# Keys and queries in pieces of two tiles, with scores from the first piece on

## The chip, the cores and the metric

The kernel runs on one core of a Trainium2 chip. The metric is the device time of one execution in microseconds; the time of a kernel is the median of its runs. The profile is one execution recorded by the hardware profiler.

## The reference

Three stages follow one another. The first is attention in blocks: 2 batches, 8 heads, 768 rows, head size 64. Each block of 32 query rows sees 8 memory rows of its own head and the keys from 16 before the block to 8 behind it.

```python
for c in range(nc):
    q_c = q[:, :, c_start:c_end]
    k_full = np.concatenate([mem_k, k[:, :, l_start:r_end]], axis=2)
    v_full = np.concatenate([mem_v, v[:, :, l_start:r_end]], axis=2)
    scores = scale * np.matmul(q_c, k_full.transpose(0, 1, 3, 2))
    a = np.exp(scores - np.max(scores, axis=-1, keepdims=True))
    a = a / (np.sum(a, axis=-1, keepdims=True) + 1e-09)
    out[:, :, c_start:c_end] = np.matmul(a, v_full)
```

Its output, as 1536 rows of 512, goes through a mixture of eight experts with two experts a row (512 to 1024 to 512, with noise on the logits), and that through a second one with one expert a row and a capacity of 384 rows. All arithmetic is in float32.

## The kernel before, in words

The order of the work is written out by hand; the engines run their instructions in the order of the program, and waits stand where data demands it. The attention treats twelve tiles of 128 rows, six a batch. The loop at L1486 calls `step(t, units)` for t from -2 to 11. Step t computes the scores of tile t+2 and subtracts their maxima (`scores`, `submax`), turns the differences of tile t+1 and takes their exponentials (`prob`), multiplies tile t with V (`attend`, `normalise`), transposes the rows of tile t-1 (`x_tr`) and makes the gate logits of tile t-2 (`logits`). Ahead of each step the loop stores the rows of the tile before (`put_x`) and issues what the table `ahead` holds for that step.

Queries and keys are needed with the head dimension on the partitions. A piece (`load_qk`, L121) is loaded by the SyncE queue, 512 KB in one transfer. Two "units" (`t_unit`, L218) turn a piece: four 128x128 transposes on TensorE into a PSUM bank, and then the copies of `t_put` (L233) into `qz` or `kt`, where the rows are put in the order in which the score matmuls read them. Q is copied by ScalarE, K by VectorE. In the kernel before, a piece is 1024 consecutive rows of four heads laid end to end (8 rows, 2 KB, a partition); four heads of 768 rows are three pieces, and a tile of all heads needs all three. So all six loads of batch 0 and their twelve units stand ahead of the first score (L1429 to L1436), and the twelve units of batch 1 are taken off a list within steps 0 to 3, as many as the table `UP` says (half of them ahead of the probabilities, half behind `normalise`). The raw pieces have six buffers.

V is loaded in groups of 128 rows with 256 B runs (`load_v`). GpSimd copies a second arrangement of it, shifted by 32 rows (`v_odd`), and the memory rows are put beside it by copies (`v_mem`) or by small transfers (`v_odd` with a queue). `v_blank` and `blank` clear what is never written. The memory keys are multiplied into place by `mem_keys`. The value matmuls of tile t (L309) read all of this for their group.

`fill` and `half_step` let the routing of the first expert stage go forward a step at a time on VectorE; it begins after step 5. At step 6 the buffers of batch 0 are given up and the first weights are loaded there (`whole0`, `PIECES`). `ZEROS` and `ZT` say ahead of which step rows of the buffers in memory are set to zero. After the attention come the expert jobs, a list of units with background work between them, up to the end of the kernel.

## Time and profile before

| What | Value |
|---|---|
| Runs (us) | 604.55, 601.17, 604.13 |
| Median (us) | 604.13 |
| The profiled execution's own time (us) | 603.3 |
| Its span (us) | 601.5 |
| TensorE busy | 581.5 us (97%) |
| VectorE busy | 370.2 us (62%) |
| ScalarE busy | 304.2 us (51%) |
| GpSimd busy | 169.8 us (28%) |
| Moved | 110.39 MB, mean 184 GB/s |

The span goes from the first to the last instruction that the profiler recorded; what of the execution lies around it is the difference to its own time. Engines are named PE (TensorE matmul), PEld (TensorE weight load, beside PE), DVE (VectorE), ACT (ScalarE), POOL (GpSimd) and SP (SyncE). A q behind the name is the engine's queue of instructions. In a row such as `psB<-ident,raw` the written tile stands first, and L223 is line 223 of the kernel. A bracket at the end of a row of the timeline gives the idle time of the engine just before it and what ended it.

### The profile page before, as it was taken

How to read it: one execution, taken by the hardware profiler on the slowest of the kernel's cores; microseconds unless marked ns; L12 is line 12 of the kernel's file. 1: busy time of each engine (PE TensorE's matmuls, PEld its weight loads, DVE VectorE, ACT ScalarE, POOL GpSimd, SP SyncE). 2: the span in 40 equal slices, each digit the busy share in tenths (PEclk: the TensorE clock that was granted, in tenths of full speed). 3: DMA queues.
4: the chain of work that ended last, by engine and by line, in shares of the span. 5: the costliest groups of instructions: out<-in, count | busy, mean ns of one | idle time of the engine just before them, and what ended most of it. 6: DMA issues, size and time to landing. Idle time of an engine off the chain costs nothing. (4 is left out here: it accounts for less than half of the span.)

```text
span 601.5 us, 12261 instructions
## 1 busy us (share of the span) xinstructions
PE 581.5 (97%) x4528; PEld 518.4 (86%) x4540; DVE 370.2 (62%) x986; ACT 304.2 (51%) x641; POOL 169.8 (28%) x244
## 2 busy tenths in 40 slices
PE   7899999999999999999999999999999999999995
PEld 4788756889999999999998898988979979878974
DVE  7788766877555555555556256373758648357571
ACT  5764633355445445445355345344327657367562
POOL 8896104135113114213040311212351111220102
PEclk9999999999999999999999999999999999999998
DMA  9996747475856758546465664554377576975741
GB/s 247 289 197 160 249 138 236 118 239 148 273 158 137 223 158 200 175 135 167 141 121 166 138 162 147 103 148 103 40 246 237 171 262 225 390 274 170 250 158 42
DMA packets 75373, 110.39 MB, mean 184 GB/s; under 512 B 28099, under 2 KB 28099, under 8 KB 75306
## 3 DMA queue, kind: packets, MB, share of 16 engines
q1 hardware_dynamic: 65866, 84.72, 45.4%
q0 software_dynamic: 9440, 24.81, 17.7%
q8 instruction: 38, 0.62, 0.4%
q14 instruction: 29, 0.24, 0.1%
HBM read 88.90 MB, written 20.48 MB: 182 GB/s over the span
## 5 line engine op out<-in xcount | busy, mean ns | idle before, releaser
L784 DVE TENSOR_TENSOR wlo<-raww,whi 128x512 fp32r<-128x512 f32 x226 | 150.2, 688 | 39.1 <-ACT whi L783 37.6
L783 ACT ACTIVATE whi<-raww 128x512 fp32r<-128x512 f32 x228 | 135.5, 623 | 5.6 <-SPq L1354 2.7
L861 DVE SCALAR_TENSOR_TENSOR hl<-psA,hh 128x256 fp32r<-128x256 f32 (+7 forms) x104 | 53.3, 513 | 75.1 <-ACT hh L860 68.9
L860 ACT ACTIVATE hh<-psA 128x256 fp32r<-128x256 f32 (+7 forms) x104 | 47.2, 454 | 99.0 <-PE psA L849 91.5
L849 PE MATMUL psA<-xh,wlo 128*128 128x256 f32 (+7 forms) x416 | 84.8, 325 | 1.5 <-issue 0.7
L849 PE MATMUL psA<-xl,whi 128*128 128x256 f32 (+7 forms) x416 | 82.2, 319 | 0.0
L849 PE MATMUL psA<-xh,whi 128*128 128x256 f32 (+7 forms) x416 | 82.2, 319 | 0.0
L1026 POOL DMA_INDIRECT x_rows<-yr,ids x25 | 39.2, 1567 | 125.5 <-ACT whi L783 82.1
L849 PEld LDWEIGHTS psA<-xh,wlo 128*128 128x128 f32 x416 | 66.4, 188 | 3.8 <-issue 1.2
L849 PEld LDWEIGHTS psA<-xl,whi 128*128 128x128 f32 x416 | 68.1, 188 | 0.5 <-DVEq L1262 0.2
L849 PEld LDWEIGHTS psA<-xh,whi 128*128 128x128 f32 x416 | 68.1, 188 | 0.3
L789 POOL DMA_INDIRECT xg<-x_rows,ids x37 | 37.4, 1010 | 109.3 <-DVE gs L1066 44.6
L849 PE MATMUL psC<-wlo,hh 128*128 128x512 f32 (+1 forms) x184 | 52.6, 406 | 0.0
L849 PE MATMUL psC<-whi,hh 128*128 128x512 f32 (+1 forms) x184 | 50.8, 395 | 0.0
L849 PE MATMUL psC<-whi,hl 128*128 128x512 f32 (+1 forms) x184 | 50.5, 394 | 0.0
L801 DVE TENSOR_TENSOR xl<-psB,xh 128x512 fp32r<-128x512 f32 (+4 forms) x33 | 21.1, 640 | 39.1 <-ACT xh L800 39.0
L849 PEld LDWEIGHTS psC<-whi,hh 128*128 128x128 f32 (+1 forms) x184 | 34.0, 186 | 8.4
L849 PEld LDWEIGHTS psC<-whi,hl 128*128 128x128 f32 (+1 forms) x184 | 34.1, 186 | 8.0
L800 ACT ACTIVATE xh<-psB 128x512 fp32r<-128x512 f32 (+4 forms) x33 | 18.3, 556 | 40.2 <-PE psB L797 37.7
L849 PE MATMUL psA<-hh,wlo 128*128 128x312 f32 (+4 forms) x160 | 36.9, 351 | 0.8 <-DVE hl L861 0.5
L1033 POOL DMA_INDIRECT out_dram<-yr,oids x12 | 12.0, 1000 | 87.5 <-ACT yr L1004 47.7
L849 PEld LDWEIGHTS psC<-wlo,hh 128*128 128x128 f32 (+1 forms) x184 | 31.9, 186 | 5.5
(366 smaller groups left out, 927.1 us busy)
## 6 DMA issues: line engine op xcount, KB each, us to landing
raww<-in_moe_w_dram SPq DMA_DIRECT2D x114, 512.0 KB
raw<-in_k_dram SPq DMA_DIRECT2D x6, 512.0 KB
raw<-in_q_dram SPq DMA_DIRECT2D x6, 512.0 KB
x_rows<-xs SPq DMA_DIRECT2D x12, 256.0 KB
out_dram<-zero SPq DMA_DIRECT2D x3, 1024.0 KB
x_rows<-zero POOLq DMA_DIRECT2D x5, 520.0 KB
v<-in_v_dram SPq DMA_DIRECT2D x10, 256.0 KB
whi<-in_moe_w_dram SPq DMA_DIRECT2D x4, 512.0 KB
```

Source lines behind the costliest of these rows:

```text
L783: nc.scalar.activation(hi[:, c], raw, AF.Copy)
L784: (eng or nc.vector).tensor_tensor(lo[:, c], raw, hi[:, c], op=OP.subtract)
L789: return nc.gpsimd.indirect_dma_start(out=xg, out_offset=None, in_=src, in_offset=bass.IndirectOffsetOnAxis(ap=ids_ap, axis=0))
L800: nc.scalar.activation(xh[:, :, o], pv[:, :, 0:n], AF.Copy)
L801: low = lambda: nc.vector.tensor_tensor(xl[:, :, o], pv[:, :, 0:n], xh[:, :, o], op=OP.subtract)
L849: nc.tensor.matmul(ps, w[a], x[b], start=first and i == 0, stop=last and i == n - 1)
L860: nc.scalar.activation(hh[:, f, 0:C], ps[:, 0:C], AF.Relu)
L861: nc.vector.scalar_tensor_tensor(hl[:, f, 0:C], ps[:, 0:C], 0.0, hh[:, f, 0:C], op0=OP.max, op1=OP.subtract)
L1026: wr = nc.gpsimd.indirect_dma_start(out=x2_d, out_offset=off, in_=yr[:n], in_offset=None, compute_op=OP.add)
L1033: wr = nc.gpsimd.indirect_dma_start(out=out, out_offset=off, in_=yr[:n, 0:DM], in_offset=None, bounds_check=N - 1, oob_is_err=False)
```

## The change

A piece is now 256 rows of all eight heads, which is two tiles, with two rows (512 B) of each head on a partition. Three pieces make a batch as before, at 512 KB each, but the scores of tile 0 and 1 need the first Q piece and the first and second K pieces alone. A unit turns four heads. Its copies are shared: half x = 0 goes to ScalarE, x = 1 to VectorE, and a K unit has four copies of 64x256 in place of two of 64x512.

Ahead of the first score stand the units of K0, Q0 and K1, and the memory keys. All other units are in the list and are taken within steps -1 to 7, two a step (three in step 3, with the memory keys of batch 1). The loads come in the order K0, memory keys, Q0, K1, memory values, V groups 0 and 1, Q1, V 2, K2, Q2, V 3, and then batch 1; the V groups of batch 1 are issued in steps 1 to 4 instead of ahead of the loop, and their second arrangement is made in steps 4 to 9 instead of 2 to 6. Raw pieces have four buffers, and two more for the last pieces of batch 1 in the other pool. The memory values of group 1 go from ScalarE to GpSimd, and one clearing of `qz` of batch 1 from GpSimd to ScalarE. The zero rows move to steps 5, 6 and 7.

```diff
-UP = (0, 0, 4, 4, 4, 1)
+UP = ((0, 0), (0, 2), (2, 0), (2, 0), (2, 0), (3, 0), (2, 0), (2, 0), (2, 0), (2, 0))
...
-RB = 6
+RB = 4
...
-ZEROS = {0: 1, 1: 1}
+ZEROS = {6: 1, 7: 1}
...
-ZT = 2
+ZT = 5
...
-        t = a0p.tile([128, 2, 8 * D], F32, name="raw", bufs=RB)
-        nc.sync.dma_start(t, bass.AP(tensor=src.tensor, offset=src.offset + (b * H * S + 1024 * i) * D,
-                                     ap=[[8 * D, 128], [HP * S * D, 2], [1, 8 * D]]))
+        last = (b, i) == (1, 2)
+        t = (asp if last else a0p).tile([128, H, 2 * D], F32, name="raw_" if last else "raw", bufs=2 if last else RB)
+        nc.sync.dma_start(t, bass.AP(tensor=src.tensor, offset=src.offset + (b * H * S + 256 * i) * D,
+                                     ap=[[2 * D, 128], [S * D, H], [1, 2 * D]]))
...
-    for w in (1, 0):
-        load_qk(0, 0, w)
+    load_qk(0, 0, 1)
     nc.sync.dma_start(memk, mem_k.rearrange("b h m d -> (b h m) d"))
-    for i in (1, 2):
-        for w in (1, 0):
-            load_qk(0, i, w)
+    load_qk(0, 0, 0)
+    load_qk(0, 1, 1)
...
+    nc.scalar.activation(qz[1][64:128, :, 0, :], warmer[64:128, None, 0:32].to_broadcast([64, HP * NC, 32]), AF.Copy)
...
-        nc.gpsimd.memset(qz[b][64:128, :, 0, :], 0.0)
+        if b == 0:
+            nc.gpsimd.memset(qz[b][64:128, :, 0, :], 0.0)
...
+        for h in range(HP):
+            nc.tensor.transpose(p[:, 128 * h:128 * h + 128], src[:, HP * a + h], ident)
...
+            act = x == 0 or (b, i, which, a) == (0, 0, 0, 1)
+            put = act_copy if act else nc.vector.tensor_copy
             if which == 0:
+                to = qz[b].rearrange("p (h c) a n -> p h c a n", h=HP)[o, :, 8 * i:8 * i + 8, a]
+                put(to.rearrange("p h c (n x) -> p x h c n", x=2)[:, x], pr)
             else:
+                for u in range(2):
+                    j = 320 * i + 16 + 24 * u + x
+                    to = kt[b][o, j:j + 1]
+                    put(bass.AP(tensor=to.tensor, offset=to.offset, ap=[list(to.ap[0]), [KW, HP], [40, 8], [2, 8]]),
+                        pr[:, :, :, 8 * u:8 * u + 8])
+            if not act:
                 fill()
...
-        some((n + 1) // 2)
+        some(n[0])
         pe_part()
-        if 0 <= t + 1 < NT:
+        if 0 <= t + 1 < NT and t:
             prob(t + 1)
         if on:
             attend(t)
             normalise(t, end)
-        some(n // 2)
+        some(n[1])
+        if t == -1:
+            prob(1)
...
+    for u in range(2):
+        t_unit(0, 0, 1, u, "BC"[u])
+    mem_keys(0)
+    for u in range(2):
+        t_unit(0, 0, 0, u, "DB"[u])
+    warm(1, "A")
+    for u in range(2):
+        t_unit(0, 1, 1, u, "CD"[u])
+    warm(1, "A")
...
+    for b, i, w in [(0, 1, 0), (0, 2, 1), (0, 2, 0)] + [(1, i, w) for i in range(3) for w in (1, 0)]:
+        raw1.append(lambda b=b, i=i, w=w: load_qk(b, i, w))
         for u in range(2):
+            units.append(lambda b=b, i=i, w=w, u=u: t_unit(b, i, w, u, "AB"[u]))
+    units.insert(8, lambda: mem_keys(1))
...
-    v_blank(1)
...
+    ahead = {-3: [*lv(0, 0, 1), *odd(0, 0, None), *mem(0), raw1[0], *lv(0, 2), *odd(0, 1, None), *mem(1), *raw1[1:3],
+                  *lv(0, 3), *odd(0, 2, nc.gpsimd), raw1[3], *lv(0, 4), raw1[4],
+                  *odd(0, 3, nc.gpsimd), gates, lambda: v_blank(1), *lv(0, 5, 6), *odd(0, 4, nc.gpsimd), *raw1[5:7], gates2,
+                  *odd(0, 5, nc.gpsimd), *raw1[7:9]],
+             1: lv(1, 0, 1), 2: lv(1, 2, 3), 3: lv(1, 4), 4: lv(1, 5, 6)}
     for g in range(G):
-        ahead.setdefault((2, 2, 3, 4, 5, 6)[g], []).extend(odd(1, g, nc.sync))
-    ahead[0] = [lambda: v_mem(0, 1, act_copy), *ahead.get(0, [])]
+        ahead.setdefault(4 + g, []).extend(odd(1, g, nc.sync))
```

## Rows read from the trace of the kernel before

**Rows 1.** The page: busy time of TensorE, and the clock granted to it by slice.

```profile
PE 581.5 (97%) x4528; PEld 518.4 (86%) x4540; DVE 370.2 (62%) x986; ACT 304.2 (51%) x641; POOL 169.8 (28%) x244
...
PEclk9999999999999999999999999999999999999998
```

**Rows 2.** Busy time by stage: stretch, its length, engines, clock, DMA share, GB/s.

```profile
4.74:15.21 10.47, 7.84 (x59) 5.68 (x59) 7.73 (x12) 6.72 (x12) 9.05 (x22) 1.00 1.12 274
15.21:19.20 3.99, 3.64 (x72) 2.75 (x73) 2.40 (x8) 2.66 (x7) 3.11 (x5) 1.00 1.05 333
19.20:25.69 6.49, 5.15 (x118) 3.99 (x119) 5.37 (x14) 4.56 (x7) 5.97 (x10) 1.00 1.10 345
...
45.80:50.07 4.27, 4.11 (x113) 3.84 (x113) 2.55 (x9) 2.09 (x8) 3.92 (x7) 1.00 0.68 167
50.07:54.34 4.27, 4.11 (x113) 3.84 (x113) 4.09 (x13) 1.62 (x5) 3.92 (x7) 1.00 0.59 163
54.34:58.93 4.59, 4.39 (x113) 3.91 (x114) 4.37 (x21) 1.41 (x5) 1.11 (x3) 1.00 0.45 100
...
81.04:601.50 520.46, 508.67 (x3036) 457.85 (x3036) 308.62 (x790) 257.35 (x532) 118.64 (x147) 1.00 0.60 176
```

**Rows 3.** Timeline of TensorE's matmuls in the opening: start, duration, line, operation.

```profile
8.43 0.66 PE L223 MATMUL psC<-ident,raw 128*128 128x128 f32 x4 [0.70 <-DMA raw<-in_k_dram]
...
13.97 0.66 PE L223 MATMUL psC<-ident,raw 128*128 128x128 f32 x4 [0.78 <-DMA raw<-in_q_dram]
...
15.21 0.92 PE L266 MATMUL psA<-kt,qz 128*64 128x64 f32 x24
```

**Rows 4.** Timeline of TensorE's matmuls in steps 0, 2, 6 and 8.

```profile
25.11 0.66 PE L223 MATMUL psB<-ident,raw 128*128 128x128 f32 x4 [1.29 <-ACT qz L216]
...
34.73 0.66 PE L223 MATMUL psA<-ident,raw 128*128 128x128 f32 x4
...
35.66 0.60 PE L336 MATMUL psD<-ident,xs 128*128 128x128 f32 x4
...
51.91 1.11 PE L309 MATMUL psC<-v,ex 64*32 64x65 f32 x64
...
58.93 1.15 PE L266 MATMUL psA<-kt,qz 128*64 128x64 f32 x32
```

**Rows 5.** The page, DMA: packets, bytes, and packets under each size.

```profile
DMA packets 75373, 110.39 MB, mean 184 GB/s; under 512 B 28099, under 2 KB 28099, under 8 KB 75306
```

**Rows 6.** Busy time in stretches of one packet size; the last column is GB/s.

```profile
3.00:5.00 2.00, 2.00 (x10) 0.88 (x9) 1.78 (x4) 0.00 (x0) 1.89 (x6) 1.00 1.05 402
8.00:11.00 3.00, 2.09 (x16) 1.71 (x17) 2.58 (x4) 1.33 (x3) 2.95 (x2) 1.00 1.04 396
34.00:40.00 6.00, 6.00 (x182) 5.64 (x171) 5.08 (x15) 4.63 (x10) 5.67 (x11) 1.00 1.27 205
```

**Rows 7.** Groups by line and shape, 4.7 to 58.93 us: busy us, mean ns.

```profile
L244 DVE COPY kt<-psA 64x512 f32<-64x512 f32 x12 | 8.2, 687 | 0.2
...
L282 DVE TENSOR_TENSOR sm<-psA,mx 128x256 f32<-128x256 f32 x10 | 4.2, 424 | 0.3
...
L216 ACT ACTIVATE v<-memv 8x1040 f32<-8x1040 f32 x2 | 2.1, 1069 | 1.8 <-POOL v L140 1.8
...
L216 ACT ACTIVATE qz<-psC 64x256 f32<-64x256 f32 x4 | 1.6, 402 | 1.3 <-PE psC L223 1.3
```

**Rows 8.** Timeline of ScalarE: its first copy of a unit.

```profile
5.38 1.29 ACT L216 ACTIVATE kt<-psB 64x512 f32<-64x512 f32 x2 [3.33 <-PE psB L223]
```

**Rows 9.** Timeline of GpSimd: its first copies of V.

```profile
15.87 2.60 POOL L140 COPY v<-v 32x520 f32<-32x520 f32 x4 [1.53 <-DMA v<-in_v_dram]
```

**Rows 10.** Timeline of SyncE's queue: V of batch 1, and the first memory rows.

```profile
31.23 8.66 SPq L134 DMA_DIRECT2D v<-in_v_dram  x7
...
43.65 3.24 SPq L143 DMA_DIRECT2D v<-memv  x4
```

**Rows 11.** Waits of SyncE's queue: total us, times, longest.

```profile
SPq L125 <- PE psD L252: 3.4, 1, 3.4
```

More of the change, by code (lines that the diff above doesn't have):

```diff
@@ L213, in mem_keys @@
                               pv[:, :, None, :].to_broadcast([128, HP, NC, NM]))
-    rest = []
     act_copy = lambda d, s: nc.scalar.activation(d, s, AF.Copy)
@@ L220, in t_unit @@
         src = raws[b, i, which]
-        pv = bank(tag).rearrange("p (r n) -> p r n", r=4)
-        for r in range(4):
-            nc.tensor.transpose(pv[:, r], src[:, a, 2 * D * r:2 * D * r + 2 * D], ident)
-        if (b, i, which) == (0, 2, 0):
-            t_put(b, i, which, a, pv, 0, 16)
-            rest.append(lambda: t_put(b, i, which, a, pv, 16, 32))
-            if a:
-                for f in rest:
-                    f()
-        else:
-            t_put(b, i, which, a, pv, 0, 32)
-    def t_put(b, i, which, a, pv, c0, c1):
+        p = bank(tag)
+        for h in range(HP):
+            nc.tensor.transpose(p[:, 128 * h:128 * h + 128], src[:, HP * a + h], ident)
         o = slice(64 * a, 64 * a + 64)
         for x in range(2):
-            pr = pv[64 * x:64 * x + 64]
-            put = act_copy if which == 0 or (b, i, a) == (0, 0, 0) else nc.vector.tensor_copy
+            pr = p[64 * x:64 * x + 64].rearrange("p (h c n) -> p h c n", h=HP, c=8)
+            act = x == 0 or (b, i, which, a) == (0, 0, 0, 1)
+            put = act_copy if act else nc.vector.tensor_copy
             if which == 0:
-                put(qz[b][o, 32 * i + c0:32 * i + c1, a].rearrange("p c (w r x) -> p x c w r", x=2, r=4)[:, x],
-                    pr.rearrange("p r (c w) -> p c w r", w=4)[:, c0:c1])
-            else:
-                base = kt[b][o, 1280 * i + 16 + x:1280 * i + 17 + x]
-                put(bass.AP(tensor=base.tensor, offset=base.offset,
-                            ap=[list(base.ap[0]), [40, 32], [24, 2], [8, 2], [2, 4]]),
-                    pr.rearrange("p r (c u w) -> p c u w r", u=2, w=2))
+                to = qz[b].rearrange("p (h c) a n -> p h c a n", h=HP)[o, :, 8 * i:8 * i + 8, a]
+                put(to.rearrange("p h c (n x) -> p x h c n", x=2)[:, x], pr)
+            else:
+                for u in range(2):
[4 more added lines that the diff above has]
+            if not act:
                 fill()
@@ L356, in step @@
         end = t == NT - 1
-        n = UP[t + 2] if t + 2 < len(UP) else 0
+        n = UP[t + 2] if t + 2 < len(UP) else (0, 0)
         def some(m):
@@ L1427, in attention_two_moe_kernel @@
     warm(WARM)
-    n = 0
-    for i in range(3):
-        for w in (1, 0):
-            for u in range(2):
-                t_unit(0, i, w, u, "BCD"[n % 3])
-                n += 1
-            warm(1, "D" if i < 2 or w else "A")
-        if i == 0:
-            mem_keys(0)
+    for u in range(2):
[7 more added lines that the diff above has]
+    warm(1, "A")
     nc.gpsimd.memset(zero, 0.0)
@@ L1439, in attention_two_moe_kernel @@
     raw1 = []
-    for i in range(3):
-        for w in (0, 1):
-            raw1.append(lambda i=i, w=w: load_qk(1, i, w))
+    for b, i, w in [(0, 1, 0), (0, 2, 1), (0, 2, 0)] + [(1, i, w) for i in range(3) for w in (1, 0)]:
+        raw1.append(lambda b=b, i=i, w=w: load_qk(b, i, w))
         for u in range(2):
-            for w in (0, 1):
-                units.append(lambda i=i, w=w, u=u: t_unit(1, i, w, u, "BA"[w]))
-    units.insert(1, lambda: mem_keys(1))
+            units.append(lambda b=b, i=i, w=w, u=u: t_unit(b, i, w, u, "AB"[u]))
+    units.insert(8, lambda: mem_keys(1))
     rev = iota([128, V], [[-1, V]], V, 0, "rev")
@@ L1495, in attention_two_moe_kernel @@
         if t == G:
-            assert not units and not ahead
             pools["a0p"].close()
```

6 lines of the change are left out of this document (2 added, 4 removed).

## The prediction

> **What bounds the kernel now.** I read the page first. TensorE is busy 97% of the span, and the granted clock stands at full speed from the first slice to the last but one, which is the upper of its two levels, 2.4 GHz [rows 1]. So the question is where TensorE still stands idle, and whether the change reaches that place. The busy time by stage answers it [rows 2]: from 81.04 us on TensorE has 508.67 us of work in 520.46 us, and nothing there is touched; what happens earlier can only bring that whole block forward or push it back. In the opening, 4.74 to 15.21 us, it is busy 7.84 of 10.47 us, and much of that is filler (L252) and transposes that wait for data. The timeline of TensorE shows why [rows 3]: transposes of the second K load begin at 8.43 us and those of the last Q load at 13.97 us, both released by a DMA, and the first scores come at 15.21 us, because a piece of 1024 flat rows covers one and a third of the four heads of a half, so that tile 0 of all heads needs all six loads (3 MB). After that TensorE is nearly full: idle 0.35, 1.34, 0.16, 0.16 and 0.20 us in the five stages shown between 15.21 and 58.93 us [rows 2], the 1.34 being one wait of 1.29 us for ScalarE's put of a Q unit [rows 4]. I take 58.93 us, the start of the scores in step 8 [rows 4], as the mark: from there on both kernels issue the same matmuls, and the shift of that mark is the gain.
>
> **The change, part by part.**
>
> *Start.* The first scores now stand in TensorE's order behind K0, the memory keys, Q0 and K1: six units and no more. K1 is the third large load in both kernels and lands at 8.43 us now [rows 3]. But its pieces are now runs of 512 B, not 2 KB. The trace has no packet between 512 B and 2 KB at all: the counts "under 512 B" and "under 2 KB" are the same [rows 5]. The bounds are the 2 KB loads at 402 and 396 GB/s (3 to 5 and 8 to 11 us) and the V loads of 256 B at 205 GB/s (34 to 40 us) [rows 6]. A straight line through the time per packet (256 B / 205 = 1.25 ns, 2048 B / 396 = 5.17 ns) gives 1.81 ns for 512 B, so about 283 GB/s; this is an estimate from these rows, and I take it. Three loads (1.57 MB) then need 5.6 instead of 4.0 us. The opening ran at 274 GB/s on the mean [rows 2], so part of it is not bound by the packets; I charge half, 0.8 us, and put K1 at 9.2 us. Two units (0.93 us, below) and one filler matmul follow, so the first scores start at about 10.6 us: **-4.6 us** (bounds: -5.4 at 396 GB/s; at 205 GB/s the three loads take 3.7 us longer, so -1.7).
>
> *Units.* Of the twelve units of the first batch six stay ahead of the scores and six go into steps -1 to 1; the second batch's twelve spread over steps 2 to 7 at two a step (three with the memory keys). Before the mark TensorE must do six units more than it did after 15.21 us. Two units take 35.66 - 34.73 = 0.93 us [rows 4]: **+2.8 us** for six.
>
> *ScalarE in step 0.* The two memory-value copies of 1.07 us each [rows 7] leave ScalarE for GpSimd. They stood ahead of the Q put on which TensorE waited 1.29 us [rows 4]. That wait goes: **-1.3 us**. GpSimd gets 2.1 us of copies and loses a blanking of 64x3072 (to ScalarE, idle 3.33 us ahead of its first put [rows 8]; by the 8x1040 copy at 1.07 us the fill takes some 3.1 us, so it fits and costs nothing; without that cover it would delay the first K put by its overrun). GpSimd's first V copies wait for V at 15.87 us now [rows 9]; with V in the queue behind K1 they start 2 to 4 us sooner, and the blanking of V for batch 1 moves behind four groups. Nothing there is on the path unless V comes late.
>
> *Puts.* A K unit was two 64x512 copies on VectorE (0.69 us each); it becomes two 64x256 on either engine. ScalarE has that shape at 0.40 us, and VectorE's nearest, 128x256, is 0.42 us [rows 7]. A Q unit goes from two ScalarE copies to one on each. The latency of a unit halves; the sum on VectorE rises a little (K and Q together from 1.38 to 1.53 us).
>
> *Early waits.* Q1 now stands behind V's first two groups and feeds the scores of step 0. On the estimates above it lands near 14 to 15 us, while TensorE, with two score sets, a filler, and one probability transpose, is ready at about 14; K2's put then keeps VectorE until after TensorE wants the scores of step 1. Two waits of about 0.7 us each, less the 0.35 us idle in that stretch now [rows 2]: **+1.0 us** (0 to 3).
>
> *Late waits.* Two things can hold steps 6 and 7. VectorE is busy 4.09 + 4.37 us of 8.86 us there [rows 2], and four units add 3.1 us: 11.6 against 10.7 us of TensorE. And the queue: all V of batch 1 is now issued in steps 1 to 4 behind the stores of x, with the memory rows of group 0 behind that, on the same SyncE queue. Now that queue ends its V issues at 31.23 + 8.66 = 39.89 us and the memory rows go out at 43.65 us [rows 10], eight us ahead of their reader at 51.91 us [rows 4]. Afterwards 6.29 MB of Q and K at 283 GB/s take 22.2 instead of 15.9 us, and four stores of 256 KB at 396 GB/s add 2.6 us. From a last V byte at about 42 us that is some 51 us, less what the queue now loses waiting for a free raw buffer (3.4 us the longest [rows 11]), which the new order of buffers avoids: 48 to 51 us. Behind a waiting memory row stand, on the same queue, the store of x, the zero rows and the first weight loads, and for the store waits VectorE, which has four buffers of x. The reader asks at about 51.91 - 4.6 - 1.3 + 1.0 + 1.9 (four of the six units) = 48.9 us. I take **+0.6 us** for both together, since VectorE catches up while TensorE waits (0 to 6). Moving the zero rows from steps 0 and 1 to 6 and 7 costs nothing: they go behind all loads of Q, K and V, and their readers come long after 81 us; without that cover they would delay the weight loads of V0 beside them by their 0.78 MB, 2 us.
>
> *Sum.* -4.6 + 2.8 - 1.3 + 1.0 + 0.6 = **-1.5 us**. The profiled execution took 603.3 us, of which the span is 601.5; so 601.8 us on its scale. The median of the three runs is 604.13, 0.8 us above it; on that scale the forecast is **602.6 us**. The 0.5% that a measurement of this kernel can tell from no change is 3.0 us.
>
> *A rule beside the row.* The 256 B rows move at 205 GB/s, about half of the 2 KB rows' 396 to 402 [rows 6], and 512 B is not in the trace. The Trainium skill, "DMA: Bandwidth & Descriptors", section "Specifications", gives 512 B as the least transfer that runs at line rate; by that the change would pay nothing for its smaller pieces, and the sum would be that of the first rival. The same page, under "Bandwidth" (why small descriptors are slow), speaks against the change: it charges every packet three fixed cycles, by which 256 B would run at 0.76 of the 2 KB rate, an estimate of 302 GB/s; the trace has 205, so the measurement decides, and I don't take 512 B as free.
>
> **The rivals.**
>
> *A: the smaller pieces cost nothing.* K1 at 8.43 us, first scores at 9.8 (-5.4), the memory rows land before they are asked for (late 0), Q1 comes earlier (early +0.3): -5.4 + 2.8 - 1.3 + 0.3 = -3.6 us, 600.5 us. For it: the opening ran at 274 GB/s even with 2 KB runs [rows 2], below my own figure for 512 B, so the packet may not be what held it. Against: V's 205 GB/s [rows 6]. Chance 0.34.
>
> *B: the load stream becomes the bound (slower).* If 512 B runs move like V's 256 B, Q and K take 30.7 us instead of 15.9. The place is the first value matmul of batch 1 (step 6, at 51.91 us now [rows 4]), which waits for the memory rows of group 0 at the end of the queue. After it two units (0.9 us) are left that the kernel before has done, so from the moment that these rows land after 51.0 us the kernel is slower, and every us later is one us lost. At 205 GB/s they land at about 42 + 14.8 + 2.6 = 59, less up to 3.4: some 5 to 7 us lost, 609 to 611 us; 0.5% slower is reached at 54.0. For it: no slack but the eight us of today, and the queue is in order. Against: twice the bytes a packet should help. Chance 0.15.
>
> *C: the time is returned in full.* TensorE's work is the same, and by 15.21 us it has done only two score sets, a probability transpose and perhaps two units (some 3.7 us) in place of six units (2.8 us); if every early wait is at its bound, 0 to -1 us, 603.5 us. It is the same side as the forecast: the two hold 0.51.
>
> **How the numbers follow.** Forecast and C together 0.51, which is "within 0.5%" (601.1 to 607.1 us); A 0.34 and with it "faster"; B 0.15 and with it "slower". The likeliest value is 602.6 us. The forecast's own range is 600.9 to 605 us. For 8 in 10 I go down through A, with the scatter of the runs, to 599.0, and up to 607.0, which leaves out most of B.
>
> **What would show it.** Right: first scores (L266 line) near 10.6 us, no wait of TensorE on ScalarE in step 0, steps 2 to 5 of about 5.2 us, and the scores of step 8 at about 57.4 us, with all later stages moved by as much. A rate of the Q and K loads near 280 GB/s in the opening confirms the packet price; near 400 it is A. A wait of the value matmuls on the DMA of the memory rows in step 6 is B, and a chain of VectorE work ahead of the probability transposes in steps 6 to 8 is the other half of the late term. The forecast is wrong if the mark moves by over 3 us either way, or if it moves as said and the time does not follow, which would mean a wait after 81 us that I have not seen.

## The result, and the profile after

Seven runs a side, on one chip:

| | before | after |
|---|---|---|
| Median (us) | 603.51 | 607.04 |
| Lowest to highest (us) | 601.17 to 604.65 | 605.37 to 607.85 |
| Profiled execution: own time, span (us) | 603.3, 601.5 | 607.85, 605.8 |
| First scores (us) | 15.21 | 10.48 |
| Scores of step 4 (us) | 41.53 | 37.45 |
| The mark, scores of step 8 (us) | 58.93 | 61.98 |

The ratio is 1.0064, 95% interval 1.0046 to 1.0081. The kernel became slower by 3.5 us where 1.5 us less was forecast, and the time lies just outside the range of 599.0 to 607.0 us.

The timeline of TensorE in the changed kernel, for the places of [rows 3, 4] (start, duration in us, instruction; the bracket is the idle time just before). Scores are the matmuls of L258; those of tile 0 and 1 come first, and then one set of 32 a step:

```profile
9.12 0.66 PE L223 MATMUL psC<-ident,raw 128*128 128x128 f32 x4 [0.70 <-DMA raw<-in_k_dram]
10.48 0.45 PE L258 MATMUL psA<-kt,qz 128*64 128x64 f32 x8
12.21 1.85 PE L258 MATMUL psA<-kt,qz 128*64 128x64 f32 x56 [1.27 <-DVE kt L236]
18.26 1.15 PE L258 MATMUL psA<-kt,qz 128*64 128x64 f32 x32 [1.14 <-DVE qz L231]
...
21.84 1.83 PE L258 MATMUL psA<-kt,qz 128*64 128x64 f32 x32
...
37.45 0.50 PE L258 MATMUL psA<-kt,qz 128*64 128x64 f32 x9
38.84 0.92 PE L258 MATMUL psA<-kt,qz 128*64 128x64 f32 x23 [0.89 <-issue]
...
55.26 1.35 PE L258 MATMUL psA<-kt,qz 128*64 128x64 f32 x26 [0.64 <-DVE kt L236]
61.98 1.15 PE L258 MATMUL psA<-kt,qz 128*64 128x64 f32 x32 [1.27 <-DVE qz L231]
...
84.29 5.38 PE L917 MATMUL psA<-whi,xf 128*128 128x512 f32 x8
```

In the kernel before, the scores of step 4 and V0, the first expert job, stand at

```profile
41.53 1.15 PE L266 MATMUL psA<-kt,qz 128*64 128x64 f32 x32
...
81.04 3.68 PE L923 MATMUL psA<-whi,xf 128*128 128x512 f32 x8
```

The start came as said: K1 at 9.12 us (forecast 9.2), first scores at 10.48 (10.6). Then come waits that the kernel before doesn't have: two for copies by VectorE in the opening, a standstill of 0.89 us within the scores of step 4 for which the trace names no releaser ("issue"), and two more for VectorE as steps 7 and 8 begin. Besides, the scores of step 1 stretch over 1.83 us instead of 1.15. The lead of 4.73 us is still 4.08 at step 4 and is 3.05 us of delay at the mark.

The windows by step, to be held against [rows 2] (us, then busy time of each engine, granted clock, DMA share, GB/s):

```profile
10.48:18.26 7.78, 5.20 (x84) 4.08 (x84) 5.96 (x15) 2.96 (x6) 6.67 (x10) 1.00 1.21 267
37.45:43.80 6.35, 5.41 (x121) 4.88 (x122) 4.65 (x18) 3.41 (x11) 1.74 (x4) 1.00 1.08 255
43.80:48.99 5.19, 5.14 (x122) 4.75 (x122) 4.14 (x12) 3.59 (x11) 4.72 (x9) 1.00 1.08 262
48.99:54.17 5.18, 5.13 (x121) 4.74 (x121) 4.94 (x16) 3.27 (x11) 4.71 (x9) 1.00 0.60 174
54.17:61.98 7.81, 5.75 (x121) 5.04 (x121) 6.76 (x27) 3.29 (x9) 1.76 (x3) 1.00 0.64 199
84.29:605.80 521.51, 510.06 (x3036) 458.54 (x3036) 308.88 (x790) 257.36 (x532) 118.90 (x147) 0.99 0.60 176
```

TensorE is idle 2.58 of 7.78 us in the first window and 2.06 of 7.81 us in step 7; in steps 6 and 7 VectorE works 11.70 of 12.99 us. Step 5 takes 5.19 us against 4.27 [rows 2]: the two units of it cost 0.92 us, as priced.

Behind the mark little changes: V0 starts 3.25 us later than in the kernel before. In this execution the granted clock fell there: V0's first eight matmuls take 5.38 us instead of 3.68, and the last window has 0.99. Not every execution has such a fall: over the whole of this one the granted clock is 0.995 on the mean, and three of the seven have 0.999 or 1.000.

**The account at the mark.** From the first scores to step 4 the new kernel does ten units, the old one twelve, and eight are left to the new one. So -4.73 - 0.93 (two units less) - 1.29 (ScalarE's wait) should make -6.95; it is 37.45 - 41.53 = -4.08, so 2.87 us of waits came in, 0.17 of it without a releaser. From step 4 to the mark the kernel before takes 17.40 us; with eight units (3.72) it should be 21.12, and it is 24.53: 3.41 us more, 0.89 of it without a releaser. In the forecast's terms: early waits 2.7 us, late waits 2.5 us, standstills without a releaser 1.06 us.

### The profile page after: what moved, and what is told of

It reads as the page before. It is cut to its first block, busy times and chain, and to the rows that moved or that the text cites. A ratio compares the mean times of both kernels' runs of the same rounds, so it can differ in the third digit from the quotient of the medians.

```text
span 605.8 us, 12293 instructions
## 1 busy us (share of the span) xinstructions
PE 584.1 (96%) x4525; PEld 520.2 (86%) x4536; DVE 372.9 (62%) x999; ACT 303.5 (50%) x647; POOL 169.4 (28%) x245
## 5 line engine op out<-in xcount | busy, mean ns | idle before, releaser
L795 DVE TENSOR_TENSOR xl<-psB,xh 128x512 fp32r<-128x512 f32 (+4 forms) x33 | 21.1, 640 | 38.9 <-ACT xh L794 38.8
```

Of the source, the lines that this page charges most:

```text
L795: low = lambda: nc.vector.tensor_tensor(xl[:, :, o], pv[:, :, 0:n], xh[:, :, o], op=OP.subtract)
```

## The experiments

Each run is the changed kernel, or the one before where that is said, with one or a few edits. The theories, by the letters that the expectations use. S: the halves of a unit interleave in one stretch of `qz` or `kt`, and VectorE's half waits for ScalarE's, so sharing is a chain through both engines. V: VectorE has more work in steps 6 to 8 than TensorE leaves it time for. R: not its amount but its order, the routing's operations ahead of the units. F: the gaps without a releaser are borders of TensorE's code. E: the early waits are VectorE's order in the opening. Against them stand P (the loads bind), G (the gaps belong to the scores) and L (Q1's landing sets the early wait). What speaks for S from the start is the timeline of VectorE in the changed kernel:

```profile
10.51 0.77 DVE L236 COPY kt<-psC 64x256 f32<-64x256 f32 x2 [0.18 <-ACT kt L216]
...
16.79 0.69 DVE L231 COPY qz<-psA 64x512 f32<-64x512 f32 x1 [0.44 <-ACT qz L216]
...
60.51 0.69 DVE L231 COPY qz<-psA 64x512 f32<-64x512 f32 x1 [0.76 <-ACT qz L216]
```

ScalarE's half at 59.90 us stands in turn behind an exponential of the routing, which waits for VectorE:

```profile
59.78 0.21 ACT L561 ACTIVATE gw<-gw 128x4 f32<-128x4 f32 x1 [1.70 <-DVE gw L560]
```

Numbers of all kernels on the changed one: the first scores, the scores of step 4, the mark, the gaps without a releaser between 20 us and the mark (those of 0.16 us and more), and "late", which is step 4 to the mark less the gaps in it (the kernel before with eight units more: 21.1, above).

| Kernel | first | step 4 | mark | gaps | late | ratio to before (95%) |
|---|---|---|---|---|---|---|
| changed | 10.48 | 37.45 | 61.98 | 1.06 | 23.6 | 1.0064 (1.0046 to 1.0081) |
| e1 | 11.25 | 38.77 | 61.55 | 1.16 | 22.5 | 1.0053 (1.0031 to 1.0075) |
| e2 | 10.65 | 37.24 | 60.09 | 0 | 22.9 | 1.0062 (1.0034 to 1.0089) |
| e6 | 10.74 | 37.54 | 61.34 | 1.17 | 22.6 | 1.0094 (1.0067 to 1.0122) |
| e7 | 10.68 | 37.87 | 61.36 | 1.07 | 22.7 | 1.0072 (1.0051 to 1.0093) |
| e8 | 10.41 | 38.15 | 61.86 | 1.90 | 22.7 | 1.0102 (1.0036 to 1.0168) |
| e9 | 10.65 | 37.20 | 62.70 | 1.98 | 21.7 | 1.0071 (1.0047 to 1.0096) |
| e10 | 10.80 | 40.64 | 63.75 | 1.35 | 23.1 | 1.0081 (1.0053 to 1.011) |
| e11 | 13.67 | 39.29 | 63.12 | 0.30 | 23.8 | 1.0107 (1.0064 to 1.0151) |
| e12 | 10.44 | 39.32 | 61.05 | 1.91 | 21.7 | 1.0061 (1.0032 to 1.0089) |
| e13 | 10.43 | 37.81 | 60.03 | 0.84 | 22.2 | 1.0040 (1.0015 to 1.0064) |
| e14 | 10.62 | 37.16 | 58.48 | 0 | 21.3 | 1.0012 (0.9986 to 1.0039) |
| e15 | 9.63 | 36.88 | 61.15 | 1.21 | 23.1 | 1.0032 (1.0011 to 1.0052) |
| e16 | 11.08 | 37.03 | 57.83 | 0.80 | 20.6 | 1.0012 (0.9989 to 1.0034) |

For e9 a fall of the clock (1.87 us, below) is taken off "late" too; e11 has one in it that makes at most 0.4 us of its mark, since VectorE's last copy for these scores ends at 62.58 us. The mark, the gaps and "late" are one execution's, the ratio that of 4 to 12 runs a kernel. How far one execution can be trusted shows where VectorE's work ahead of the mark is as in the changed kernel: "late" is 23.1 in e10 and e15, 23.4 to 23.8 in e11 and 23.6 in the changed kernel.

### Whole units, and the units ahead of the routing

In e1 each engine copies a whole unit:

```diff
-            act = x == 0 or (b, i, which, a) == (0, 0, 0, 1)
+            act = a == 0
```

> The changed kernel, but with a unit's copies on one engine: the unit of heads 0 to 3 on ScalarE, that of heads 4 to 7 on VectorE, instead of one half x each. The number of copies on an engine is the same. The mark is the start of the scores in step 8: 58.93 us in the kernel before, 61.98 us in the changed one. Theory S (in the changed kernel VectorE's copy of a unit waits until ScalarE's copy of the same unit is done, because the two interleave in one stretch of qz or kt, so the sharing makes a chain and not a halving): the waits of VectorE on ScalarE in front of its copies (0.44 us at 16.79 us, 0.76 us at 60.51 us) go, the mark comes 1 to 1.5 us earlier, the time falls by as much, to about 605.8 us. Theory R (the routing's instructions in steps 6 and 7 stand in front of the copies): the mark moves by less than 0.5 us. Theory P (the loads bind): no change.

In e2 `half_step()` stands behind `some(n[0])`:

```diff
-        half_step()
         some(n[0])
+        half_step()
```

> The changed kernel, but in each step the units of the list are taken ahead of the routing's half step instead of behind it. Theory R (VectorE's copies of K in step 6 and ScalarE's and VectorE's of Q in step 7 wait behind routing instructions, which cost the scores of steps 7 and 8 0.64 and 1.27 us and more in their engines' lag): steps 6 and 7 shrink to about 5.2 us each, the mark comes about 2 us earlier, to 60 us, the time falls to about 605 us. Theory V (VectorE has too much work in steps 6 and 7 whatever the order): the routing is pushed back instead, the mark moves by 1 us at most and step 8 or 9 grows by what step 7 loses. Theory P: no change.

In e1 the stretch from first scores to the mark is 50.30 us against 51.50: 1.2 us less by one edit that takes no work away (with the gaps taken off both it is 1.3), and the wait at the mark falls from 1.27 to 0.38 us:

```profile
61.55 1.15 PE L258 MATMUL psA<-kt,qz 128*64 128x64 f32 x32 [0.38 <-DVE qz L231]
```

So S is a part. In e2, steps 7 and 8, by windows (columns as above):

```profile
53.25:60.09 6.84, 5.27 (x122) 4.79 (x122) 6.48 (x25) 2.52 (x7) 2.16 (x4) 1.00 0.70 231
60.09:67.18 7.09, 6.39 (x119) 5.08 (x121) 4.76 (x25) 3.78 (x13) 0.00 (x0) 0.76 0.79 252
```

VectorE works 6.48 of 6.84 us ahead of the mark, whichever comes first, and the scores of step 8 wait for it all the same, 1.52 us. The mark came 1.9 us earlier, near the 60 us of theory R, but 1.06 of that only because this execution has no gaps; "late" is 22.9 against 23.6. So the order explains 0.7 us at most, and V stands. Behind the wait of 1.52 us the clock fell (0.76 in step 8, which takes 7.09 us instead of 5.02), and the lead was lost again.

### Two terms tried alone on the kernel before

In e4 the kernel before has the memory values of group 1 on GpSimd and the clearing of `qz` of batch 1 on ScalarE, as in the change:

```diff
-    ahead[0] = [lambda: v_mem(0, 1, act_copy), *ahead.get(0, [])]
```

> The kernel before, with one part of the change alone: the memory values of group 1 of batch 0 are copied by GpSimd instead of ScalarE, and ScalarE clears the lower half of qz of batch 1 at the start instead of GpSimd. The forecast's third term (the wait of 1.29 us on ScalarE's Q copy in step 0 goes): the mark comes 1.3 us earlier, at about 57.6 us, 602.2 us. Rival: GpSimd has 2.1 us more to do ahead of the second group's arrangement, which then holds the value matmuls of steps 1 or 2: no gain, 603.5 us.

In e5 it loads Q and K in 512 B runs (`ap=[[2 * D, 128], [S * D, H], [1, 2 * D]]`), whose rows stand in other places than the copies take them from:

> The kernel before, with the loads of Q and K in runs of 512 B (two rows of each of eight heads a partition) instead of 2 KB, the same bytes in the same order; all else is left, so Q and K rows are mixed up in the attention. Theory P (the price of the smaller packets): six loads ahead of the first scores take 3.1 MB x (1/283 - 1/396) = 3.2 us more, the first scores start at 18.4 instead of 15.21 us, the mark moves by 2 to 4 us, the time to about 606.5 us. Rival (the opening is not bound by packets; K1 of the changed kernel came only 0.69 us later than before): the first scores move by 1 us or less, the time stays within 1 us.

e4: 602.75 against 602.44 us, ratio 1.0 (0.9979 to 1.0021). The first scores come 0.88 us earlier, the wait on ScalarE in step 0 is gone and that step shorter by 1.5 us, but the mark is at 58.69, only 0.24 us earlier; step 1 has a gap of 1.01 us without a releaser, step 2 a DMA wait of 0.38. So the term of -1.3 was a true wait, and its going is not seen in the time. e5: 607.68 us, ratio 1.0095 (1.0065 to 1.0125), 5.2 us more, of which the mark, 2.73 us later, explains half. The first scores come 0.83 us later, and the value matmuls of step 3 wait 1.47 us for their memory rows, up to 41.46 us: a wait of rival B's kind, but for rows of batch 0 and in the old order of loads. In the changed kernel the place that B names is free: the first value matmuls of batch 1 start at 51.74 us without a wait. It is not free by much: in e2, where they start at 50.71 us, they wait 0.26 us for the memory rows.

### VectorE in steps 6 to 8

Four ways to take work off VectorE in the steps ahead of the mark: e6 gives the last pieces' copies to ScalarE, e7 makes the routing's constants four steps later, e8 has the last four units in steps 4 and 5, e9 is e6 and e7. The three edits, one below the other:

```diff
-            act = x == 0 or (b, i, which, a) == (0, 0, 0, 1)
+            act = x == 0 or (b, i) == (1, 2) or (b, i, which, a) == (0, 0, 0, 1)
...
+        if t == G + 4:
             y_consts()
...
-UP = ((0, 0), (0, 2), (2, 0), (2, 0), (2, 0), (3, 0), (2, 0), (2, 0), (2, 0), (2, 0))
+UP = ((0, 0), (0, 2), (2, 0), (2, 0), (2, 0), (3, 0), (2, 2), (2, 2))
```

> The changed kernel, with the copies of the last Q and K pieces of batch 1 (steps 6 and 7) all on ScalarE instead of half on VectorE. It takes about 2.9 us of copies off VectorE in 54 to 62 us. Theory V (VectorE has more work in steps 6 to 8 than TensorE, and that is the late loss): step 7 loses its 1.27 us wait for VectorE, step 8 doesn't grow in return, the mark comes 2 to 3 us earlier (59 to 60 us instead of 61.98), the time is 604 to 605 us. Theory S alone (only the chain of the two shared copies delays the scores): step 7 is shorter by 1 to 1.3 us and step 8 the same, mark near 60.7. Rival R (the time is set elsewhere, by GpSimd or a transfer): the mark stays within 0.5 us of 61.98.

> The changed kernel, with the routing's constants (the four VectorE instructions of y_consts, 2.0 to 2.4 us) made four steps later, in step 10 instead of step 6. Theory V: as they lie in the stretch in which VectorE is full, the mark comes about 2 us earlier (near 60 us), and the 2 us return in step 10 only as far as VectorE is full there too. Theory S: the mark moves by under 0.5 us, since the copies still wait for ScalarE. Rival R: no move. Time by V 605, by the others 606 to 607 us.

> The changed kernel, with the last four units of batch 1 in steps 4 and 5 instead of 6 and 7, two more behind the normalisation in each. Steps 4 and 5 hold 0.93 us more of TensorE's work each, steps 6 and 7 as much less. Theory V: VectorE is not full in steps 4 and 5 (4.65 and 4.14 us of work in 6.35 and 5.19 us), so steps 6 and 7 come to about 4.3 us, the scores of step 8 no longer wait, and the mark is near 60 us. If the load stream is late after all (the last pieces not there by about 45 us), TensorE waits for a DMA in step 5 and the mark is at 62 us or later. Time by V 605 us.

> The changed kernel with both edits: the last copies on ScalarE and the routing's constants in step 10. Together some 5 us less VectorE work before the mark. Theory V: no wait of TensorE for VectorE in steps 6 to 8, mark near 58.5 to 59.5 us (the kernel before: 58.93), time 603 to 604 us. Theory S: as with the copies alone. Rival R: the mark stays near 62 us.

"Late" falls from 23.6 to 22.6, 22.7 and 22.7 us by one edit each, and to 21.7 by two, near 21.1. A single edit stands just below the 23.1 to 23.8 of the kernels without one; two together are clear of them, and e12 repeats their 21.7. So V is shown, with about half of what was expected of a single edit, since the next wait takes over (in e6 the scores of step 8 wait 0.80 us for ScalarE, in e8 the value matmuls of step 7 wait 0.88 us). But the marks came 0.6 us earlier at most, and none of the four times is lower than that of the changed kernel (1.0071 to 1.0102 of before against 1.0064). For e9 the timeline says why:

```profile
37.20 0.51 PE L258 MATMUL psA<-kt,qz 128*64 128x64 f32 x9
39.69 0.92 PE L258 MATMUL psA<-kt,qz 128*64 128x64 f32 x23 [1.98 <-issue]
40.53 1.12 PE L223 MATMUL psA<-ident,raw 128*128 128x128 f32 x4
41.44 1.06 PE L223 MATMUL psB<-ident,raw 128*128 128x128 f32 x4
```

and its windows of one us (the third number from the right is the granted clock):

```profile
38.00:39.00 1.00, 0.00 (x0) 0.00 (x0) 0.19 (x2) 1.00 (x5) 0.00 (x0) 1.00 1.14 318
...
41.00:42.00 1.00, 1.00 (x7) 1.00 (x6) 0.97 (x3) 0.31 (x2) 0.29 (x1) 0.50 1.04 291
42.00:43.00 1.00, 1.00 (x6) 0.74 (x5) 0.97 (x4) 0.81 (x4) 0.93 (x2) 0.50 1.14 260
43.00:44.00 1.00, 1.00 (x16) 0.67 (x18) 0.94 (x3) 0.32 (x2) 0.90 (x2) 0.52 1.26 224
```

TensorE stands still for 1.98 us, and then its clock is at the lower of its two levels, 1.2 GHz, until about 44 us: transposes that take 0.66 us at full clock take 1.12. Step 4 costs 9.04 us in place of some 5.2.

### The gaps without a releaser

Where TensorE's instructions are as many as in the changed kernel, they stand behind the 6th or 7th score matmul of step 3, the 9th of step 4, the 13th of step 5 and the 22nd of step 7, in kernels with other times. From gap to gap TensorE has nearly the same number of instructions. These are the windows from one gap to the next in the changed kernel (32.35 us to 38.83) and over two such distances in e6 (44.01 to 55.87), with matmuls and weight loads in the first two brackets:

```profile
32.35:38.83 6.48, 5.46 (x127) 4.92 (x126) 4.79 (x13) 3.46 (x11) 4.83 (x10) 1.00 0.79 218
```

```profile
44.01:55.87 11.86, 11.09 (x251) 10.06 (x251) 10.46 (x35) 8.72 (x26) 10.76 (x18) 1.00 0.78 213
```

That is 253 in the one, twice 251 in the other. Between 30 and 60 us the DMA view of the changed kernel lists

```profile
q8 instruction: 5, 0.08, 1.2%
```

which are five transfers of 16 KB of instructions. The Trainium skill, "Runtime: NRT & Kernel Launch", section "Instruction fetch mechanics", says that the code is refilled in blocks of 256 instructions; the recorded counts are a little under that. The same section of the Trainium skill calls the cost of such a border mostly hidden; the gaps here were up to 1.98 us. e10 moves the code, in time that TensorE has anyway:

```diff
-    warm(WARM)
+    warm(WARM - 3)
+    short = bank("D")
+    for _ in range(21):
+        nc.tensor.matmul(short[:, 0:32], warmer[:, 0:128], warmer[:, 0:32], start=True, stop=True)
```

> The changed kernel, with three of the ten filler matmuls of the opening replaced by 21 short ones of 32 columns: 18 matmuls (36 instructions with their weight loads) more on TensorE before the first unit, in time that it has anyway. Every instruction of TensorE behind them stands 36 places later in its stream. Theory F (the gaps without a releaser lie at the borders of blocks of TensorE's code, of which one comes over the instruction queue every 256 instructions): the gap that stood behind the 6th score matmul of step 3 and behind the 9th of step 4 goes to a place 18 matmuls earlier in the program, into the transposes of x or the logits (or isn't seen there, since these instructions are four times as long); no gap behind the 9th matmul of step 4. Rival G (the gap belongs to the scores, through what they read or write): it stays behind the 6th and the 9th. Time: by F 605 to 606 us if the longer instructions hide the border, by G 606 to 607 us.

TensorE in e10:

```profile
31.10 0.33 PE L328 MATMUL psD<-ident,xs 128*128 128x128 f32 x1
32.78 0.49 PE L328 MATMUL psD<-ident,xs 128*128 128x128 f32 x3 [1.35 <-issue]
33.10 0.96 PE L338 MATMUL psD<-wg,xt 128*128 128x18 f32 x8
34.00 1.66 PE L258 MATMUL psA<-kt,qz 128*64 128x64 f32 x32
```

The gap now stands behind the first transpose of x, 17 matmuls ahead of where it was (6 + 3 + 8). e11, with 15 matmuls more, has it between these transposes and the logits, 14 ahead:

```profile
33.01 1.07 PE L338 MATMUL psD<-wg,xt 128*128 128x18 f32 x8 [0.30 <-issue]
```

So the gap goes with the place in the code: F is right and G is out. That the longer instructions would hide the border was wrong: it lasted 1.35 us, the clock fell behind it, and the time is 606.51 us, ratio 1.0081. How long a border lasts changes from profile to profile, from nothing seen (e2, e14) to 1.98 us; with one profile a kernel it isn't shown whether that goes with the kernel or with the execution. What sets the length stays open: in e10 the DMA moved 36 GB/s on the mean in the gap, so busy transfers alone don't. Whether the changed kernel has more of it than the one before isn't shown either: by the same count the kernel before has 0, e4 1.2 and e5 0.3 us, of which 0.2 and 0.3 stand ahead of probability transposes, where the kernel before has the same 0.16 us with a releaser named (0.16 of the 0.80 us of e16 stand there too).

### What the early start is worth

e11 puts 15 more filler matmuls ahead of the first scores (`warm(16, "A")` in place of `warm(1, "A")`).

> The changed kernel, with 15 more filler matmuls ahead of the first scores (3.2 us of TensorE's time at 0.22 us each, of which the wait of 1.27 us that stands there hides a part): the second tile's scores end 1.8 us later than 14.06 us. It asks what the early start is worth at the mark. If the losses behind it are chains of work (theories S and V), the mark is 1.5 to 2 us later, near 63.7 us, and the time 608 to 609 us. If the start is given back anyway, by something that stands at a time of its own (the loads, the code), the mark stays within 0.5 us of 61.98 and the time at 606 to 607 us. By F the gaps move too, 15 matmuls earlier in the program.

The second tile's scores end at 15.75 us (13.67 + 2.08), 1.69 later; the mark is 1.14 us later. This execution has 0.76 us less of gaps, and in step 7 the clock fell behind a wait of 0.92 us, with at most 0.4 us at the mark (above):

```profile
56.22 1.98 PE L258 MATMUL psA<-kt,qz 128*64 128x64 f32 x26 [0.92 <-DVE kt L236]
```

That leaves 1.5 of the 1.69 us. The time goes from 1.0064 to 1.0107 of before, 2.6 us, with a wide interval (four runs) that overlaps that of the changed kernel. By the mark, then, nearly nothing that stands at a time of its own gives the start back: what is gained there counts, and is lost in the waits behind it.

### Together, up to a version without the losses

e12 is e9 with e10's shift. e13 has whole units (e1), the constants later (e7) and the shift; e14 besides the last units in steps 4 and 5 (e8).

> The changed kernel with the last copies on ScalarE, the routing's constants in step 10 and the 18 extra short matmuls. Without the 1.98 us gap and the fall of the clock behind it, the kernel with the first two edits would have had its mark at 58.9 us (62.70 - 1.98 - 1.87). Theories V and F together: mark at 59 to 60 us, time 603 to 604 us. If the time stays at 605.5 to 606.5 us with an early mark, something behind the mark takes it back; if the mark is at 61 to 62.5 us, it is another wait than these in steps 3 to 8.

> The changed kernel with a whole unit to one engine (first four heads to ScalarE, last four to VectorE) in place of half of each, the routing's constants in step 10 and the 18 extra short matmuls. Theory S: the chain through both engines goes, so the scores of steps 0, 7 and 8 wait less: from the first scores to the mark 48.5 to 49.5 us (51.50 in the changed kernel, 50.30 with whole units alone), mark near 60, time 603.5 to 604.5 us. If only V counts, it is like the edit of the constants alone: 50.7 us, 605 to 606 us.

> The kernel of the whole units, the later constants and the 18 short matmuls, and besides the last four units of batch 1 in steps 4 and 5 instead of 6 and 7. In that kernel one wait for VectorE is left ahead of the mark, 0.90 us in step 7. Theory V: that wait goes, steps 6 and 7 come to 4.3 to 4.6 us, the mark is 0.5 to 1 us earlier (59.0 to 59.5 us where no gap at a border of the code is longer than 0.84 us), the time 603 to 603.5 us against 604.26, so within 0.4% of the kernel before. Rival: the four units' copies collide with the copies and normalisations of steps 4 and 5 instead, and the mark stays near 60 us, or the loads of the last pieces come after 40 us and TensorE waits for a DMA in step 5.

e12: late 21.7 as in e9, but 1.91 us of gaps, 1.39 of it at one border in step 2; the mark is at 61.05 (59.1 without the gaps) and the time 605.49 us, two us above what was expected. The border moved and was not hidden, as in e10. e13: mark 60.03, 604.26 us; from first scores to the mark 49.60, S and V together. e14: the wait of 0.90 us in step 7 is gone, and the windows from step 4's end on are

```profile
43.88:49.95 6.07, 6.07 (x131) 5.62 (x130) 5.05 (x16) 4.17 (x12) 5.54 (x10) 1.00 1.13 253
49.95:54.22 4.27, 4.27 (x115) 3.84 (x114) 3.77 (x12) 2.45 (x6) 3.86 (x8) 1.00 0.65 199
54.22:58.48 4.26, 4.26 (x114) 3.83 (x113) 3.98 (x18) 1.42 (x5) 1.43 (x3) 1.00 0.59 146
```

TensorE doesn't stand still once in three steps, the mark is at 58.48 us, and the time 602.62 us against 602.06: ratio 1.0012 (0.9986 to 1.0039). No loss can be told any more, though up to 0.4% is not excluded: the shared copies and the amount of VectorE's work ahead of the mark are the late half, and the borders, of which this execution shows none, come on top.

### The packets alone

e15 is the changed kernel with loads in 2 KB runs, for its time alone.

```diff
-        nc.sync.dma_start(t, bass.AP(tensor=src.tensor, offset=src.offset + (b * H * S + 256 * i) * D,
-                                     ap=[[2 * D, 128], [S * D, H], [1, 2 * D]]))
+        nc.sync.dma_start(t.rearrange("p (a h) n -> p a (h n)", a=2), bass.AP(tensor=src.tensor, offset=src.offset + (b * H * S + 1024 * i) * D,
+                                     ap=[[8 * D, 128], [HP * S * D, 2], [1, 8 * D]]))
```

> The changed kernel with the Q and K loads in runs of 2 KB as in the kernel before, everything else as changed (the rows then stand in other places, so that the attention computes with keys and queries mixed up: this run is for its time alone). Step 'start': the second K piece lands at 8.4 to 8.6 us instead of 9.12, the first scores come 0.5 to 0.7 us earlier. If the small packets also set the early and the late waits (the loads) or the gaps at the borders of TensorE's code (the queue of the instructions behind them), these shrink too: mark at 59.5 to 60.5 us, time 604 to 605 us. If the waits are work on VectorE and ScalarE (S and V), they stay: mark 61.3 to 61.5 us, time 606 us. The reverse edit on the kernel before cost 2.7 us at the mark, most of it in one DMA wait that the changed order doesn't have.

```profile
8.09 0.66 PE L223 MATMUL psC<-ident,raw 128*128 128x128 f32 x4 [0.52 <-DMA raw<-in_k_dram]
...
9.63 0.45 PE L258 MATMUL psA<-kt,qz 128*64 128x64 f32 x8
11.23 1.85 PE L258 MATMUL psA<-kt,qz 128*64 128x64 f32 x56 [1.16 <-DVE kt L236]
```

K1 lands 1.03 us earlier and the first scores come 0.85 earlier; the mark is 0.83 earlier (61.15). The waits for VectorE stay (1.16 in the opening, 0.96 at the mark), and so does a border of 1.21 us in step 4: neither is the packets' doing, and P is out as their cause. The time, 1.0032 (1.0011 to 1.0052), is lower by 1.9 us, of which the mark explains 0.83; the rest is not explained, and the interval overlaps that of the changed kernel.

### The early waits

e16 is e14 with Q1's units ahead of the maxima of tile 1, and the probabilities of tile 1 behind the scores of tile 2. These units also use other PSUM banks (C and D). The part that moves the units:

```diff
             scores(t + 2)
+            if t == -1:
+                some(2)
             submax(t + 2)
```

> The kernel before this one in the series (whole units, later constants, last units in steps 4 and 5, 18 short matmuls), and besides the two units of Q1 ahead of the maxima of tile 1 in VectorE's order, and the probabilities of tile 1 behind the scores of tile 2. Theory E (the early wait is VectorE's order: two maxima at 1.5 us each and then the copies of Q1, from the end of the first scores on, while its data is there): Q1's copies end near 16.4 us instead of 17.9, the scores of step 0 start at 16.5 us instead of 18.04, and as the probabilities of tile 1 (0.5 us) follow later, the mark is some 1 us earlier, near 57.4 us, the time 601 to 602 us, equal to or just below the kernel before. Rival L (Q1's landing sets it): its transposes wait for the DMA from 14.0 us on and the scores of step 0 stay at 17.5 us or later; mark unchanged at 58.5, time 602 to 603 us.

Timeline of VectorE in e16, then of TensorE:

```profile
14.52 0.82 DVE L274 TENSOR_TENSOR sm<-psA,mx 128x256 f32<-128x256 f32 x3
15.56 1.39 DVE L231 COPY qz<-psD 64x512 f32<-64x512 f32 x2 [0.22 <-PE psD L223]
16.98 0.69 DVE L271 TENSOR_REDUCE mx<-psA 128x8 f32<-128x512 f32 x1
```

```profile
12.64 1.85 PE L258 MATMUL psA<-kt,qz 128*64 128x64 f32 x56 [1.11 <-DVE kt L236]
17.10 1.15 PE L258 MATMUL psA<-kt,qz 128*64 128x64 f32 x32 [0.28 <-DVE qz L231]
```

From 12.64 to the scores of step 0 it is 4.46 us, against 5.86 in e14 (12.18 to 18.04). Q1's transposes waited for no DMA: E is right, L is out. The mark is at 57.83 us, 1.1 ahead of the kernel before, although the first scores came 0.46 later than in e14. The time is 602.11 against 601.02 us, ratio 1.0012 (0.9989 to 1.0034): no gain that can be told. Of the 1.1 us, 0.37 are left where V0 begins (80.67 against 81.04 us); between the two places TensorE waits longer for VectorE, once 0.64 us where the kernel before has 0.27. And the clock fell in the profiled execution; the timeline of V0's first matmuls in e14 and then in e16 shows the price:

```profile
80.88 3.68 PE L917 MATMUL psA<-whi,xf 128*128 128x512 f32 x8
```

```profile
80.67 5.38 PE L917 MATMUL psA<-whi,xf 128*128 128x512 f32 x8
```

## Why the prediction was wrong, by its own steps

The terms for the start, the units and ScalarE's wait came out. The step that failed is the price of the waits: early waits put at +1.0 and measured as 2.7 us, late waits put at +0.6 and measured as 2.5 us, and 1.06 us of standstills that were not in the sum at all. The waits were priced copy by copy, with a unit's latency halved, where VectorE's whole order of work and its waits for ScalarE set them. Together that is 4.7 us more than was charged, which turns the -1.5 into some +3; the mark shows +3.05.

**Start, -4.6: right** for the first score matmul, which it was about. It is -4.73. But only the first 8 of the 64 matmuls begin there; the other 56 wait until 12.21 us for VectorE's copies of K1, which this term doesn't price (below). The price of the 512 B runs, charged at 0.8 us, is 1.03 us at K1 by e15 (8.09 us; the thirteen profiles of this order with 512 B runs have 9.12 to 9.57). From 3 to 5 us the changed kernel moves 321 GB/s and e15, with 2 KB runs, 395; the estimate for 512 B was 283. The Trainium skill, "DMA: Bandwidth & Descriptors", section "Specifications", gives 512 B as the least size at line rate; 321 against 395 GB/s does not agree with that, and rival A's condition did not hold.

**Units, +2.8: right,** 0.92 us for two in step 5.

**ScalarE in step 0, -1.3:** the wait is gone as said; alone on the kernel before it gave no time that can be measured (e4).

**Puts.** "The latency of a unit halves" failed. VectorE's half waits for ScalarE's, so a unit's copies end after both, and where ScalarE is held by something else (the exponential of the routing, in step 7) VectorE is held with it. Undone alone, it gave 1.2 us up to the mark (e1).

**Early waits, +1.0 (0 to 3): 2.7 us.** The forecast had two waits of 0.7 us, for Q1 in step 0 and for K2 in step 1. The second came as said: the scores of step 1 take 0.68 us too long, and VectorE copies K2 until 22.61 us in the middle of them (the link is read from these times; the trace names this copy for 0.2 us alone). The first is 1.14 us, and not for the landing: Q1's transposes begin at 15.45 us without a wait for a DMA. What TensorE waited for was a sum on one engine: from 13.36 us on, VectorE has two rounds of maxima and differences of about 1.5 us each and two copies of 0.69, and between them 0.44 us of waiting for ScalarE; that ends at 18.20 us. TensorE, whose first scores end at 14.06 us, has 3.06 us of work until the scores of step 0. e16 shows it by moving the copies forward. A third wait, 1.27 us for K1's copies in the middle of the first scores, the forecast put at nothing; it is read from the trace, and no run tests it by making these copies faster (e11 only covers it with filler). The three make 3.1 us, less the 0.35 of before.

**Late waits, +0.6 (0 to 6): 2.5 us.** The place and the engine were right: 11.6 us of VectorE work against 10.7 of TensorE was the prediction's own sum, and 11.70 was measured in steps 6 and 7. What failed is "VectorE catches up while TensorE waits": the two steps took 12.99 us, so VectorE itself stood still for 1.29 of them, more than half of that in the wait of 0.76 us for ScalarE ahead of the mark. The copies stand in order between maxima, normalisation and routing, so nothing was caught up ahead of the scores that needed them. The other half, the queue (rival B), did not happen: the first value matmuls of batch 1 found their memory rows. B had the side right (slower), but not the place; and the landing times that it gives, 55.6 to 59 us, would make its loss 4.6 to 8 us, not 5 to 7.

**Not in the sum:** the borders of TensorE's code, 1.06 us in this execution. Rival C, the gain returned in full by early waits, comes nearest in kind; the return went past zero because the late half came on top.

**Why the times follow the marks so loosely.** One reason is the clock. The mean granted clock over the runs is 0.9943 for e6 and 0.9978 for the kernel before measured beside it; 0.0035 of 605 us is 2.1 us. In e14 it is 0.9976 against 0.9973. For the changed kernel itself it is 0.9971, like the 0.9969 of the kernel before beside e1, and the run of the changed kernel with a granted clock of 1.000 took 606.39 us: there the clock is no part of the 3.5 us that can be seen.

## What to carry to other kernels

Price a copy by the work that stands ahead of it in its engine's order, from the moment its input exists, and not by its duration; the engine whose sum over two or three steps passes TensorE's sets the pace even when its mean share is low (62% here). Here the halves of a unit's copies lay within one another in one stretch, and splitting them over two engines cost 1.2 us against a whole unit to each engine. Price the copies behind the first transposes too, and not only the landing of the data: they held 56 of the first 64 score matmuls for 1.27 us. An early start is worth what the next engine in the chain can take up.

## What the runs showed of the hardware

TensorE's code arrives in blocks (16 KB a transfer; 251 to 253 recorded instructions from gap to gap), and a border cost up to 1.98 us in a kernel that is otherwise full; 18 matmuls more ahead of it moved the gap 17 matmuls earlier in the program (e10), 15 more moved it 14 (e11). Behind standstills of 0.92 (e11), 1.35 (e10), 1.52 (e2) and 1.98 us (e9) the granted clock fell from full speed, 2.4 GHz, to half of it; in the last three some 1.4 to 1.9 us were lost each time. Behind 1.21 (e15), 1.39 (e12) and 1.47 us (e5) it did not fall. In six of the fourteen profiles with the changed order (changed, e2, e7, e12, e13, e16) it also fell at V0's first matmuls, with no standstill over 0.4 us in the ten us before, and in none of the three with the order of before (before, e4, e5). So the length of the last standstill alone doesn't tell, and what does stays open.
